# Decode attention beside an MLP on one core: scores by 128-row matmuls, softmax bank by bank, diagonal sums on VectorE

## The chip, the cores and the metric

The kernel runs on 1 core of a Trainium2 chip. Time is the device time of one execution in microseconds (us). Before the change, three runs gave 216.44, 219.92 and 221.33, with a median of 219.92. One execution was recorded by the hardware profiler, and all durations below are from it. Engines are named as in the profile: PE (TensorE), PEld (its weight loads), DVE (VectorE), ACT (ScalarE), POOL (GpSimd), SP (the queue that issues nearly all DMAs).

## The reference

```python
xn = layernorm(x)                                   # x: 4 rows of 576, bf16
# A: decode attention, batch 4, 32 query heads on 16 key heads, window = the last 2048 of 8192 positions
q = (xn @ wq) as 4 x 32 x 128
p = softmax(q @ k^T * 128 ** -0.5) over the window
a = (p @ v) as 4 x 4096 @ wo
# B: MLP; with a sequence of one, the shifted groups g0..g3 are all zero, so x1 = xn
b = xn + gelu(layernorm(xn) @ w3) @ w4              # 576 -> 4608 -> 576
out = x + a + b
```

K and V of the window are 16 heads of 2 MB each. With wq, w3, wo and w4 the kernel reads 87.2 MB and writes 4.5 KB.

## The kernel before

**Layout.** A K or V tile of one head h holds all four batch rows: partition b*32 + p holds 64 consecutive positions (NCH = 64) of batch b, 128 values each. So one load is 128 partitions of 16 KB. K must be turned before it can be contracted over the 128 values: DVE does this with two STREAM_TRANSPOSE per head (line 258), which turn 32x32 blocks of 32-bit words. The result kt has the 128 values of a key spread over four places, the 32 partitions of a group g and the four places y inside, so a score is a sum over four y; the four groups g of 32 partitions hold different keys.

**Scores.** qz holds q for these 32x32 products: per batch b, head h and place y a block of 32 columns that is zero except in the two columns of that head's two query heads. For each head, y and b there are four matmuls (line 267), one for each group g, of 32 rows by 32 columns, each into a bank of its own S[g], rows 32*b and up. So 64 matmuls a head write into the same four PSUM banks for all 16 heads; a row of S[g] is a pair of batch and query head. Nothing of the scores can be read before the last head.

**q.** wq is multiplied by the normalised x in five pieces (line 204) into two PSUM tiles; eight DVE and eight ACT casts (lines 222, 224) put q into q_rows; for each y, eight PE transposes (line 230) go into a PSUM tile tq, and four copies, one for each b, put tq into qz: even b on DVE (line 239), odd b on ACT (line 237). tq has two buffers.

**Softmax.** After the last head of K: a maximum of each bank on DVE (279), Exp of each bank on ACT (283), then four pieces. In each piece E is multiplied by the reciprocal of its row's sum and by a mask of its batch row (300 on ACT, 302 on DVE), turned by PE in two halves (306), and copied from PSUM into PZ, first half on DVE (314), second half on ACT (311).

**V.** For head h, 16 matmuls (line 331) with PZ stationary, 128x32, and V moving, 128x512, fill a bank; four neighbouring key blocks i stand beside each other, so that only the diagonal (i with i) of the four 32x(4*128) row groups counts. ACT copies the bank to osb (line 356). In a later step, `select`, four f32 matmuls against sel pick and add the diagonal (line 362, shown as eight instructions), then DVE casts `on` (366), four small matmuls (369) and two casts `onx` (377) spread the head for wo. After each second head, `project` adds that pair's product with wo to ACC (line 339). `select` and `project` are put into a list `later` and run before the next head's V matmuls.

**MLP.** w3 is multiplied beside the first five heads of K (line 401), gelu follows, and w4's first nine rows of 128 come after K; the remaining 27 come at the end, in loads of 9, 9, 4, 2, 2 and 1 rows (line 419).

**Buffers and order.** SP issues the loads in one queue and waits there for a free buffer. K and V share the pool `kv` with NKV = 6 tiles. The pool `w` has three slots, for pieces of wq, w3, w4 and for E. `kt` has two slots, for kt, q_rows, the softmax pieces and osb. `wo` has three. qz and PZ share one buffer (`pzp`). PSUM has eight banks: ps_tp 1, ps_s 4 (S, before them qp, after them the softmax's transposes), ps_o 2, ps_acc 1. The order of instructions within an engine's queue is set by the framework's planner, from the order in the program, priorities and its own estimate of times; so the order in a trace can differ from the order of the lines. The planner also makes all the waits, and it puts those that touch the same PSUM tile behind one another.

Of the kernel before, what the change touches and what calls it, by code (L numbers as in the profile page):

```python
# [9 lines left out]
ALU = mybir.AluOpType  # L10
# [6 lines left out]
NKV = 6  # L17
# [4 lines left out]
def kernel(  # L22
# [13 lines left out]
):  # L36

# [36 lines left out]
    def ap_of(t, offset_elems, dims):  # L74
        a = t[:]
        return bass.AP(a.tensor, a.offset + offset_elems, [list(a.ap[0])] + [list(d) for d in dims])

    def ap32(t, offset, dims):
        names = " ".join("abcdefg"[:len(t.shape) - 1])
        a = t[:].rearrange(f"p {names} -> p ({names})").bitcast(I32)  # L80
        return bass.AP(a.tensor, a.offset + offset, [list(a.ap[0])] + [list(d) for d in dims])
# [5 lines left out]
    pzp = ctx.enter_context(tc.tile_pool(name="pz", bufs=1))  # L87
# [3 lines left out]
    ps_s = ctx.enter_context(tc.tile_pool(name="ps_s", bufs=4, space=PSUM))  # L91
# [73 lines left out]
    NH = Hkv * rep  # L165
    qz = pzp.tile([P, B, Hkv, NY, NH], BF16, tag="pz", name="qz")

# [7 lines left out]
    nq = B * Hkv * NY * NH // 4  # L175
# [50 lines left out]
    for y in range(NY):  # L226
# [5 lines left out]
        for b in range(B):  # L232
            src = ap_of(tq, b, [[G, 4], [rep * P, 4], [P, rep]])
            step = NY * NH + rep
            dst = ap_of(qz, b * Hkv * NY * NH + y * NH, [[4 * step, 4], [step, 4], [1, rep]])
            if b % 2:
                nc.scalar.copy(out=dst, in_=src)
            else:
                nc.vector.tensor_copy(out=dst, in_=src)
# [10 lines left out]
    S = []  # L250

    def k_scores(h):
# [8 lines left out]
        if h == 0:  # L261
            S.extend(ps_s.tile([P, 512], F32, tag="S", name=f"S{g}") for g in range(NG))
        for y in range(NY):
            e, t = divmod(y, 2)
            for b in range(B):
                for g in range(NG):
                    nc.tensor.matmul(out=S[g][32 * b:32 * b + 32, :].rearrange("p (c k l) -> p c k l", k=GK, l=2),  # L267
                                     lhsT=qz[32 * g:32 * g + 32, b, h, y, :],
                                     rhs=kt[32 * g:32 * g + 32, :, e, b:G:B, :, t],
                                     start=(h == 0 and y == 0), stop=(h == Hkv - 1 and y == NY - 1),  # L270
                                     skip_group_check=True)

    def softmax():
        E = wpl.tile([P, NCH, NG, GK], F32, tag="w", name="E")
        mx = const.tile([P, NG], F32)
        nb = const.tile([P, 1], F32)
        sm = const.tile([P, NG], F32)
        for g in range(NG):
            nc.vector.reduce_max(out=mx[:, g:g + 1], in_=S[g][:], axis=AX.X)  # L279
        nc.vector.reduce_max(out=nb[:], in_=mx[:], axis=AX.X)  # L280
        nc.vector.tensor_scalar_mul(out=nb[:], in0=nb[:], scalar1=-scale)  # L281
        for g in range(NG):
            nc.scalar.activation(out=E[:, :, g, :].rearrange("p (c l) k -> p c k l", l=2),  # L283
                                 in_=S[g][:].rearrange("p (c k l) -> p c k l", k=GK, l=2), func=ACT.Exp, bias=nb[:], scale=scale, accum_out=sm[:, g:g + 1])
        rd = const.tile([P, 1], F32)
        nc.vector.tensor_reduce(out=rd[:], in_=sm[:], op=ALU.add, axis=AX.X)
        nc.vector.reciprocal(out=rd[:], in_=rd[:])
        rdm = const.tile([P, B], F32)
        nc.vector.tensor_scalar_mul(out=rdm[:], in0=mask[:], scalar1=rd[:])  # L289

        PZ = pzp.tile([P, Hkv, NCH, B * rep], BF16, tag="pz", name="PZ")
        HC = CP // 2
        for piece in range(NP):
            c0 = piece * CP
            pr = ktp.tile([P, CP, NG, GK, B], BF16, tag="kt", name=f"pr{piece}")
            for b in range(B):
                src = E[:, c0:c0 + CP, :, :].rearrange("p c g k -> p (c g k)")
                dst = pr[:, :, :, :, b].rearrange("p c g k -> p (c g k)")
                if b == 3 or (b == 1 and piece % 2):
                    nc.scalar.mul(out=dst, in_=src, mul=rdm[:, b:b + 1])  # L300
                else:
                    nc.vector.tensor_scalar_mul(out=dst, in0=src, scalar1=rdm[:, b:b + 1])  # L302
            for half in range(2):
                tp = ps_s.tile([P, HC, P], BF16, tag="S", name=f"pt{piece}{half}")
                for cc in range(HC):
                    nc.tensor.transpose(out=tp[:, cc, :],  # L306
                                        in_=pr[:, half * HC + cc, :, :, :].rearrange("p g k b -> p (g k b)"),
                                        identity=ident[:])
                c1 = c0 + half * HC
                if half:  # L310
                    nc.scalar.copy(out=ap_of(PZ, c1 * B * rep, [[NCH * B * rep, Hkv], [rep, HC * B], [1, rep]]),  # L311
# [119 lines left out]
    for h in range(Hkv):  # L431
# [7 lines left out]
        if h in w3:  # L439
            g_piece(w3.pop(h), h)  # L440
            if h == KJ:
                gelu()
# [63 lines left out]
```

## Time and profile before

| | before |
|---|---|
| median of the three runs, us | 219.92 |
| profiled execution, us | 216.28 |
| its span, us | 214.4 |
| mean granted clock of PE | 0.729 |
| PE busy, us | 129.1 (60%) |
| DVE busy, us | 109.1 (51%) |
| ACT busy, us | 30.3 (14%) |
| moved by DMA | 87.45 MB, 408 GB/s over the span |
| instructions | 4295 |
| K transposes, line 258 | 32 of 2293 ns |
| score matmuls, line 267 | 1024, 36.9 us busy |
| V matmuls, line 331 | 256, 30.1 us busy |
| select matmuls, line 362 | 128, 23.5 us busy |

The span goes from the first to the last instruction of the profiled execution; its time is 1.9 us longer. A line of the table of groups gives the source line, engine, operation, tile written and tiles read, shapes and count, then busy time and the mean of one, then the idle time just before them and what ended it. The slices cut the span into 40 parts of 5.36 us and give busy tenths. The stages by time: q until 33 us, K until 113, softmax until 134.5, V until 205, the rest of w4 until 211.4.

### The profile page before, as it was taken

Reading aid. Unit: us, or ns where it says so; the run is one execution under the profiler, and the core shown is the slowest. Engines: PE = TensorE matmul, PEld = TensorE weight load, DVE = VectorE, ACT = ScalarE, POOL = GpSimd, SP = SyncE. Lnnn points to the kernel's source line nnn. Section 1 sums busy time; section 2 is a strip of 40 time slices with the busy share of each in tenths; the row PEclk is TensorE's granted clock in tenths of the full one; section 3 lists DMA queues with packets and bytes.
Section 4 is the critical chain, followed back from the end, with each engine's and each line's share of the span. In section 5 each row is a group of like instructions: output and inputs, shape, how many; then the busy total and the mean of one; then the engine's idle time right before and its main releaser. Section 6 shows DMA issues by size and latency. Waiting matters only on the chain.

```text
span 214.4 us, 4295 instructions
## 1 busy us (share of the span) xinstructions
PE 129.1 (60%) x1937; PEld 75.8 (35%) x1937; DVE 109.1 (51%) x157; ACT 30.3 (14%) x52; POOL 1.8 (1%) x8
## 2 busy tenths in 40 slices
PE   0343787847644445444534086886777876877694
PEld 0110743526411111111101073555545453545383
DVE  7941968583999999999885493111100000000000
ACT  0201320000000000000002897221111112011200
POOL 1110000000000000000000000000000000000000
PEclk9999999678558587575558569969675558555859
DMA  6999999999999999999999999999999999999980
GB/s 253 433 407 426 426 432 426 415 433 437 411 425 419 437 425 425 419 431 425 413 433 428 428 420 427 424 426 409 432 429 427 419 424 428 431 416 418 422 324 33
DMA packets 8251, 87.45 MB, mean 408 GB/s; under 512 B 924, under 2 KB 1064, under 8 KB 2728
## 3 DMA queue, kind: packets, MB, share of 16 engines
q1 hardware_dynamic: 8216, 87.17, 96.7%
q8 instruction: 15, 0.25, 0.5%
q14 instruction: 4, 0.03, 0.0%
q10 hardware_dynamic: 16, 0.01, 0.0%
HBM read 87.17 MB, written 0.00 MB: 407 GB/s over the span
## 4 chain that ended last, share of the span: by engine, by line
DMA 40%; PE 33%; DVE 15%; ACT 8%; issue 3%; SPq 0%; ACTq 0%; DVEq 0%
DMA t<-in_A_k_cache_dram 36%; PE OT L362 11%; PE O L331 11%; DVE kt L258 6%; PE ACC L339 5%; ACT osb L356 4%; DMA wq<-in_A_wq_dram 3%; PE pt L306 2%; ACT E L283 2%; PE OT L369 2%; DVE qz L177 2%; PE qp L204 1%; ACT PZ L311 1%; ACT pr L300 1%; DVE mx L279 1%
## 5 line engine op out<-in xcount | busy, mean ns | idle before, releaser
L258 DVE STREAM_TRANSPOSE kt<-t 128x2048 int32<-128x2048 int32 x32 | 72.3, 2293 | 12.3 <-DMA t<-in_A_k_cache_dram 12.3
L267 PE MATMUL S<-kt,qz 32*32 32x512 bf16 x1024 | 36.9, 625 | 37.5 <-DVE kt L258 36.1
L366 DVE CAST on<-OT 128x8 bf16<-128x8 f32 x16 | 2.7, 166 | 58.4 <-PE OT L362 58.4
L267 PEld LDWEIGHTS <-qz 32*32 32x32 bf16 x1024 | 10.7, 95 | 60.1 <-issue 56.9
L331 PE MATMUL O<-t,PZ 128*32 128x512 bf16 x256 | 30.1, 506 | 1.1 <-ACT PZ L311 0.6
L362 PE MATMUL OT<-sel,osb 128*128 128x8 f32 x128 | 23.5, 311 | 10.2 <-ACT osb L356 10.1
L362 PEld LDWEIGHTS OT<-sel,osb 128*128 128x128 f32 x128 | 22.1, 260 | 20.5 <-ACT osb L356 20.0
L356 ACT COPY osb<-O 128x512 f32<-128x512 f32 x16 | 9.3, 586 | 59.4 <-PE O L331 59.4
L331 PEld LDWEIGHTS <-PZ 128*32 128x32 bf16 x256 | 10.5, 112 | 8.2 <-issue 3.6
L283 ACT ACTIVATE E<-S,nb 128x512 f32<-128x512 f32 x4 | 4.0, 1115 | 59.4 <-DVE nb L281 59.4
L306 PE MATMUL pt<-ident,pr 128*128 128x128 bf16 x64 | 5.8, 266 | 9.6 <-DVE pr L302 8.6
L401 PEld LDWEIGHTS <-w 128*128 128x128 bf16 x144 | 9.2, 163 | 5.2 <-DMA w<-in_B_w_dram 2.7
L401 PE MATMUL ACC<-ln2T,w 128*128 128x4 bf16 x144 | 9.6, 202 | 1.8 <-DMA w<-in_B_w_dram 1.8
L339 PE MATMUL ACC<-wo,onx 128*4 128x288 bf16 x64 | 8.8, 418 | 2.6 <-DVE onx L377 2.6
L306 PEld LDWEIGHTS <-pr 128*128 128x128 bf16 x64 | 5.0, 122 | 10.9 <-ACT pr L300 10.8
L377 DVE CAST onx<-OT 32x16 bf16<-32x16 f32 x32 | 5.3, 165 | 6.0 <-PE OT L369 5.8
L300 ACT ACTIVATE pr<-E,rdm 128x512 bf16<-128x512 f32 x6 | 8.1, 1434 | 0.7 <-DVE rdm L289 0.7
L204 PE MATMUL qp<-wq,xnT 128*4 128x512 bf16 x32 | 4.0, 620 | 5.1 <-DMA wq<-in_A_wq_dram 5.1
L302 DVE TENSOR_SCALAR pr<-E,rdm 128x512 bf16<-128x512 f32 x10 | 6.5, 797 | 0.3 <-PE pt L306 0.2
L339 PE MATMUL ACC<-w,gT 128*4 128x288 bf16 x72 | 6.6, 341 | 0.0
L224 DVE CAST q_rows<-qp 128x256 bf16<-128x256 f32 x8 | 2.9, 411 | 7.0 <-PE qp L204 7.0
L369 PE MATMUL OT<-on,ident 128*32 128x8 bf16 x64 | 4.2, 172 | 3.6 <-DVE on L366 3.6
(71 smaller groups left out, 64.4 us busy)
## 6 DMA issues: line engine op xcount, KB each, us to landing
t<-in_A_k_cache_dram SPq DMA_DIRECT2D x16, 2048.0 KB, 24.7
t<-in_A_v_cache_dram SPq DMA_DIRECT2D x16, 2048.0 KB, 28.4
w<-in_B_w_dram SPq DMA_DIRECT2D x4, 1152.0 KB, 12.8
wo<-in_A_wo_dram SPq DMA_DIRECT2D x8, 576.0 KB, 18.2
wq<-in_A_wq_dram SPq DMA_DIRECT2D x4, 1024.0 KB, 6.7
w<-in_B_w_dram SPq DMA_DIRECT2D x3, 1296.0 KB, 27.8
w_t<-in_B_w_dram SPq DMA_DIRECT2D x1, 576.0 KB, 14.0
w<-in_B_w_dram SPq DMA_DIRECT2D x1, 576.0 KB, 25.2
```

Of the source, the lines that this page charges most:

```text
L258: nc.vector.transpose(out=ap32(kt, e * G * 2, [[2 * G * 2, NCH // 2], [1, 2], [2, G]]), in_=ap32(kn, e * G, [[2 * 2 * G, NCH // 2], [2 * G ...
L267: nc.tensor.matmul(out=S[g][32 * b:32 * b + 32, :].rearrange("p (c k l) -> p c k l", k=GK, l=2), lhsT=qz[32 * g:32 * g + 32, b, h, y, :], ...
L283: nc.scalar.activation(out=E[:, :, g, :].rearrange("p (c l) k -> p c k l", l=2), in_=S[g][:].rearrange("p (c k l) -> p c k l", k=GK, l=2), ...
L300: nc.scalar.mul(out=dst, in_=src, mul=rdm[:, b:b + 1])
L302: nc.vector.tensor_scalar_mul(out=dst, in0=src, scalar1=rdm[:, b:b + 1])
L306: nc.tensor.transpose(out=tp[:, cc, :], in_=pr[:, half * HC + cc, :, :, :].rearrange("p g k b -> p (g k b)"), identity=ident[:])
L331: nc.tensor.matmul(out=bank[G * j:G * j + G, :], lhsT=PZ[:, h, c0:c0 + NI, :].rearrange("p c m -> p (c m)"), rhs=vn[:, c0:c0 + NI, :].rear ...
L339: nc.tensor.matmul(out=ACC[32 * q:32 * q + B, 0:DH], lhsT=lhsT, rhs=rhs_cols(q * DH, (q + 1) * DH), start=False, stop=False, skip_group_ch ...
L356: nc.scalar.copy(out=osb[:], in_=bank[:])
L362: nc.tensor.matmul(out=OT[:, 0:rep * B], lhsT=osb[:, i * Dh:(i + 1) * Dh], rhs=sel[:, i * rep * B:(i + 1) * rep * B], start=(i == 0), stop ...
L369: nc.tensor.matmul(out=T[0:32, x, :], lhsT=ident[:, x:P:XR], rhs=on[:].rearrange("p r b -> p (r b)"), start=(x == 0), stop=(x == XR - 1), ...
L401: nc.tensor.matmul(out=gp[:, fc, :], lhsT=lhsT, rhs=rhs, start=False, stop=False, skip_group_check=True)
```

## The change

- **Scores.** qz now has, for each b, h and y, a block of 32 columns in which group g's rows are non-zero only in columns 8*g to 8*g+7. One matmul of 128 rows by 32 columns then gives all four groups at once, each in its own eight rows of the output. Eight rows are four heads with two query heads each, so a PSUM bank is one set of four heads (HG = 4) and 512 columns, and 16 matmuls a head take the place of 64. Writing qz takes 16 copies for each y, of 32 partitions each, in the place of four of 128 partitions.
- **Softmax by bank.** A bank of four heads is complete when its last head is scored. Its softmax has three steps: `softmax_exp` (maximum, Exp), `softmax_spread` (reciprocal of the sum, multiply by the masks), `softmax_turn` (16 PE transposes, 16 copies to PZ[bk]). They are called one, two and three heads later in the program; for the last bank they are called before V's heads 0, 1 and 2. A row's keys now stand in four rows (one for each g), so the maximum and the sum go over them by `over_g`: a DVE transpose, a reduce, a broadcast and a transpose back. Multiplies and copies are on ACT for the first three banks and shared with DVE for the last.
- **Diagonal sums.** osb and the four f32 matmuls become four DVE operations from the PSUM bank into osum (128x128), with `diag` as the per-row factor, and one f32 matmul.
- **Memory.** NKV is 5 where it was 6; qz and the PZ[bk] have memory of their own; E and its product share one tile EP in the pool `w`; PSUM has ps_s 2 and a new ps_t with one tile of two banks.

```diff
-NKV = 6
+NKV = 5
...
-    ps_s = ctx.enter_context(tc.tile_pool(name="ps_s", bufs=4, space=PSUM))
+    ps_s = ctx.enter_context(tc.tile_pool(name="ps_s", bufs=2, space=PSUM))
+    ps_t = ctx.enter_context(tc.tile_pool(name="ps_t", bufs=1, space=PSUM))
...
+    HG = 4
+    NB = HG * rep
+    qz = const.tile([P, B, Hkv, NY, G], BF16)
...
-        for b in range(B):
-            src = ap_of(tq, b, [[G, 4], [rep * P, 4], [P, rep]])
-            step = NY * NH + rep
-            dst = ap_of(qz, b * Hkv * NY * NH + y * NH, [[4 * step, 4], [step, 4], [1, rep]])
-            if b % 2:
-                nc.scalar.copy(out=dst, in_=src)
-            else:
-                nc.vector.tensor_copy(out=dst, in_=src)
+        for g in range(NG):
+            p0 = slice(32 * g, 32 * g + 32)
+            for b in range(B):
+                src = ap_of(tq, b, [[G, HG], [rep * P, HG], [P, rep]], p0)
+                dst = ap_of(qz, (b * Hkv * NY + y) * G + NB * g, [[HG * NY * G, HG], [NY * G + rep, HG], [1, rep]], p0)
+                if b % 2:
+                    nc.scalar.copy(out=dst, in_=src)
+                else:
+                    nc.vector.tensor_copy(out=dst, in_=src)
...
+        bk, h4 = divmod(h, HG)
+        if h4 == 0:
+            S[bk] = ps_s.tile([P, 512], F32, tag="S", name=f"S{bk}")
         for y in range(NY):
             e, t = divmod(y, 2)
             for b in range(B):
-                for g in range(NG):
-                    nc.tensor.matmul(out=S[g][32 * b:32 * b + 32, :].rearrange("p (c k l) -> p c k l", k=GK, l=2),
-                                     lhsT=qz[32 * g:32 * g + 32, b, h, y, :],
-                                     rhs=kt[32 * g:32 * g + 32, :, e, b:G:B, :, t],
...
+                nc.tensor.matmul(out=S[bk][32 * b:32 * b + 32, :].rearrange("p (c k l) -> p c k l", k=GK, l=2),
+                                 lhsT=qz[:, b, h, y, :], rhs=kt[:, :, e, b:G:B, :, t],
+                                 start=(h4 == 0 and y == 0), stop=(h4 == HG - 1 and y == NY - 1),
+                                 skip_group_check=True)
+
+    def over_g(col, op, last):
+        t1 = small.tile([P, G], F32, tag="og1")
+        nc.vector.transpose(out=t1[:].bitcast(I32), in_=col[:].bitcast(I32))
+        r = small.tile([P, NB], F32, tag="og2")
+        nc.vector.tensor_reduce(out=r[:], in_=t1[:].rearrange("p (g m) -> p m g", m=NB), op=op, axis=AX.X)
+        t2 = small.tile([P, NG, NB], F32, tag="og3")
+        last(t2, r[:].unsqueeze(1).to_broadcast([P, NG, NB]))
+        t3 = small.tile([P, G], F32, tag="og4")
+        nc.vector.transpose(out=t3[:].bitcast(I32), in_=t2[:].rearrange("p g m -> p (g m)").bitcast(I32))
+        return t3[:, 0:1]
...
+    def softmax_exp(bk):
+        nc.vector.reduce_max(out=cols[0][:, 0:1], in_=S[bk][:], axis=AX.X)
+        nb = over_g(cols[0], ALU.max, lambda t, r: nc.vector.tensor_scalar_mul(out=t[:], in0=r, scalar1=-scale))
+        EP = wpl.tile([P, 512 + NCH * GK * B // 2], F32, tag="w", name=f"EP{bk}")
...
+        nc.scalar.activation(out=SM[bk][0].rearrange("p (c l k) -> p c k l", l=2, k=GK),
+                             in_=S.pop(bk)[:].rearrange("p (c k l) -> p c k l", k=GK, l=2),
+                             func=ACT.Exp, bias=nb, scale=scale, accum_out=cols[1][:, 0:1])
+
+    def softmax_spread(bk):
+        E, pr = SM[bk]
+        rd = over_g(cols[1], ALU.add, lambda t, r: nc.vector.tensor_copy(out=t[:], in_=r))
...
+        for b in range(B):
+            if bk < Hkv // HG - 1 or b == 3:
+                nc.scalar.mul(out=pr[:, :, b], in_=E, mul=rdm[:, b:b + 1])
+            else:
+                nc.vector.tensor_scalar_mul(out=pr[:, :, b], in0=E, scalar1=rdm[:, b:b + 1])
+
+    def softmax_turn(bk):
...
+        tp = ps_t.tile([P, NCP, P], BF16, tag="T", name=f"pt{bk}")
+        for c in range(NCP):
+            nc.tensor.transpose(out=tp[:, c, :], in_=prc[:, c * P:(c + 1) * P], identity=ident[:])
+        PZ[bk] = const.tile([P, HG, NG, NCP, NB], BF16, name=f"PZ{bk}")
+        n = 0
+        for i in range(NG):
+            for g in range(NG):
+                pi, po = slice(32 * i, 32 * i + 32), slice(32 * g, 32 * g + 32)
+                if bk == Hkv // HG - 1 and n % 3 < 2:
+                    nc.vector.tensor_copy(
...
                 else:
+                    nc.scalar.copy(
...
-        osb = ktp.tile([P, NI * Dh], F32, tag="kt", name=f"osb{h}")
-        nc.scalar.copy(out=osb[:], in_=bank[:])
+        osum = ktp.tile([P, Dh], F32, tag="kt", name=f"osum{h}")
+        nc.vector.tensor_scalar_mul(out=osum[:], in0=bank[:, 0:Dh], scalar1=diag[:, 0:1])
+        for i in range(1, NI):
+            nc.vector.scalar_tensor_tensor(out=osum[:], in0=bank[:, i * Dh:(i + 1) * Dh], scalar=diag[:, i:i + 1],
+                                           in1=osum[:], op0=ALU.mult, op1=ALU.add)
...
-            for i in range(NI):
-                nc.tensor.matmul(out=OT[:, 0:rep * B], lhsT=osb[:, i * Dh:(i + 1) * Dh],
-                                 rhs=sel[:, i * rep * B:(i + 1) * rep * B],
...
+            nc.tensor.matmul(out=OT[:, 0:NB], lhsT=osum[:], rhs=sel[:], start=True, stop=True, skip_group_check=True)
...
+        for d, step in enumerate((softmax_exp, softmax_spread, softmax_turn), 1):
+            if h >= d + HG - 1 and (h - d) % HG == HG - 1:
+                step(h // HG - 1)
...
-    PZ = softmax()
+    steps = [softmax_exp, softmax_spread, softmax_turn]
     for v in range(Hkv):
...
+        if steps:
+            steps.pop(0)(Hkv // HG - 1)
         v_compute(v)
```

## The prediction

> **What bounds the kernel now.** I read the page's slices first. They show which resource is full from end to end.
>
> ```profile
> DVE  7941968583999999999885493111100000000000
> ACT  0201320000000000000002897221111112011200
> PEclk9999999678558587575558569969675558555859
> DMA  6999999999999999999999999999999999999980
> GB/s 253 433 407 426 426 432 426 415 433 437 411 425 419 437 425 425 419 431 425 413 433 428 428 420 427 424 426 409 432 429 427 419 424 428 431 416 418 422 324 33
> ```
>
> The 16 DMA engines are full from the second slice to the last but one, at some 425 GB/s. The 20 us from 114 to 134 in which DVE and ACT make the softmax and PE does little are no dip in that row: V is loading then. 87.45 MB at 425 GB/s are 205.8 us of a span of 214.4. What is left is 2 us before the first packets, an uneven last 4 us, and 3 us from the last packet to the end. A faster engine therefore earns nothing in the middle; what counts is whether a wait ever lets the DMA queue run empty, and what follows the last byte.
>
> Next the chain of waits in order of time, for the second half.
>
> ```profile
> 134.55 0.41 PE O L331 x2
> ...
> 192.97 0.59 ACT osb L356
> 193.56 0.04 issue
> 193.61 1.89 PE OT L362 x8
> ...
> 205.64 5.74 PE ACC L339 x60
> 211.40 0.45 DVE fin L473
> ```
>
> From 134.5 to 211.4 PE and its hand-overs to ACT and DVE run without one wait for a transfer. So there are two bounds at par: the stream, and a PE chain that starts 20 us late. The windows by 1 us show how near they are:
>
> ```profile
> 209.00:210.00 1.00, 1.00 (x17) 0.96 (x14) 0.00 (x0) 0.00 (x0) 0.00 (x0) 0.79 0.38 144
> 210.00:211.00 1.00, 1.00 (x21) 0.99 (x18) 0.00 (x0) 0.00 (x0) 0.00 (x0) 1.00 0.09 31
> 211.00:212.00 1.00, 0.35 (x6) 0.03 (x1) 0.45 (x1) 0.00 (x0) 0.00 (x0) 1.00 0.00 0
> ```
>
> The last columns are granted clock, DMA share and GB/s: bytes move until 210 to 211 (the last w4 load, issued at 195.05, lands 15.8 us later, at 210.9), and the last matmul that needs them starts at 211.1. PE is at most 0.5 us behind.
>
> **The V stage on PE.** The timeline has an osb copy at 178.46 and one at 188.09, two heads apart: 9.63 us per pair. The stream needs 2 x 2048 + 576 KB = 4.78 MB per pair, 11.2 us at 427 GB/s. The edit: osb (0.59) becomes four DVE operations on 128x128 (nearest rows: 128x144 copy from PSUM 0.27, two-input 128x144 0.31), 1.1 to 1.25 per head, +1.3 per pair at the upper end; the 8 f32 L362 instructions, 1.06 in one head of a pair and 1.88 in the other by the granted clock, become 2, 0.27 and 0.47: -2.2. New pair: 8.7 us, under 11.2. V also starts some 18 us earlier, so PE is going to wait for V, with the stream the only bound.
>
> The granted clock in this stage is 0.54 to 0.66 by 10 us windows with PE 75% busy, and 0.50 in the slow stretches. If all of it ran like the slow heads, before's pair would grow by 0.82 (L362) and 1.1 (the 16 L331, 0.92 against 1.76 for twelve) to 11.6: over the stream. Its PE has no spare time at the end, so that comes through whole: an execution that got a colder clock would be up to 8 x 1.9 = 15 us longer. The medians fit this: 219.92 and 221.33 stand 3.6 and 5.0 over the profiled 216.28. The new pair in such a run is 8.7 + 0.2 + 1.1 = 10.0, still hidden.
> The Trainium skill (TensorE: Matmul & The Clock Gate, Part 1) says that an array left idle for a window of about 3.4 us falls back to half clock. That speaks against a change that lets PE wait for V; by it every new pair is the 10.0 one, by the trace's mixture 8.7.
>
> **The K stage.** Scores: 64 matmuls a head on 32x32 become 16 on 128x32 like L331 (16 take 1.2 to 2.3 us), before 2 x 1.13; PE waits 36 us for DVE there, so nothing comes of it. DVE is what is near its limit: 4.51 us of transposes per head against 4.9 between K tiles. The rows:
>
> ```profile
> L258 DVE STREAM_TRANSPOSE kt<-t 128x2048 int32<-128x2048 int32 x32 | 72.3, 2293 | 12.3 <-DMA t<-in_A_k_cache_dram 12.3
> L356 ACT COPY osb<-O 128x512 f32<-128x512 f32 x16 | 9.3, 586 | 59.4 <-PE O L331 59.4
> L300 ACT ACTIVATE pr<-E,rdm 128x512 bf16<-128x512 f32 x6 | 8.1, 1434 | 0.7 <-DVE rdm L289 0.7
> ```
>
> Each of three banks adds to DVE a maximum (L279, 0.68) and ten small operations; 0.16 to 0.23 each by L280 to L289 (small 32-column transposes have no row: between the slope of L258, 1.1 ns per column, 0.04, and a 128x128 reduce, 0.30; I take 0.16). About 2.5 us a bank, 2 to 4. Idle time from 58 us on is 5.1 us for two of them: DVE ends K at most 1 to 3 us later (112.6 before), and this is bought back many times by the softmax that leaves. ACT gets, per bank, Exp 1.3, four L300 = 5.7 and 16 copies of 32x512 (L356, and half of L311's 1.07: 0.53 to 0.59) = 9: 16 us in the 19.6 of four heads. It was idle. If ACT were late, PE would wait for its transposes and K tiles pile up; three queued tiles (15 us) cover that.
>
> **Buffers.** NKV 6 to 5: load n waits for tile n-5. When that tile is transposed, or used by V, three later ones are still queued, 15 us of stream against 1.3 us from an issue to the first bytes (the first load is issued at 0.73; the window from 1 to 2 us moves 50 GB/s, the next 315). I cost it at nothing (0 to 1 us). Before, after V5 was issued at 116.1 the next V load waited for V0's use until 135; now V0 is used some 4 us after it lands at about 113. EP takes w slots; the slots w4 needs were used by banks that are long done. The last bank's 16 copies alternate engines on one tile: 11 x 0.4 + 5 x 0.56 = 7 us and hand-overs, 8.5 at most; only head 12 needs them, 60 us later, and the heads held up meanwhile have 15 us of V in the queue.
>
> **The start.** q's copies are the one place where the new work can starve the stream.
>
> ```profile
> 29.69 0.19 DVE L239 COPY qz<-tq 128x32 bf16<-128x32 bf16 x1 [1.22 <-PE tq L230]
> 29.91 0.19 ACT L237 COPY qz<-tq 128x32 bf16<-128x32 bf16 x1 [1.23 <-DVE qz L239]
> 30.13 0.19 DVE L239 COPY qz<-tq 128x32 bf16<-128x32 bf16 x1 [0.25 <-ACT qz L237]
> 30.36 0.19 ACT L237 COPY qz<-tq 128x32 bf16<-128x32 bf16 x1 [0.26 <-DVE qz L239]
> ```
>
> Copies from one tq tile wait for each other in turn, 0.215 apart; two tq tiles side by side at 27.77 gave 0.115. 16 copies become 64, so 48 more: 5.6 to 10.3 us. K0's scores then end at 40 to 45 and not at 34.8, and with them g_piece(1) and the load of w3_t and K5 behind it on SP's queue, issued at 38.78. By then SP has issued 19.92 MB; the first seven slices moved 15.02 MB by 37.5, so the rest lasts 11.5 us, to 49.0. Spare: 10.2, less 1.3 to the first bytes. At 5.6 nothing is lost; at 10.3, 1.4 us. I take 0, keeping 1.4 as an end.
> The Trainium skill (PSUM — Partial Sum Buffer, Terms) says that different 32-partition quadrants of one bank may be accessed at the same time. The new copies go by quadrants, so by it they need not alternate and, as an estimate, 24 of 0.18 us on each of two engines add 4.3 us; the trace shows only whole-height copies, and those take turns.
>
> **The sum.** Instruction loads (queue 8) take 0.5% of 16 engines' span, 1.07 us for 4295 instructions. 768 matmuls and 768 weight loads of the scores and 192 of L362 go, some 150 small ones come: 37% fewer, -0.4. PE's lag behind the last load: -0.2 (0 to -0.5). Span 214.4 - 0.6 = 213.8; with the 1.9 that the profiled time has over its span, **215.7**. This stands 0.3% under the profiled 216.28 and 1.9% under the median of 219.92, for if the stream alone sets the time, runs should come together there. A difference of about 2% is what a measurement of this kernel can tell from none; this forecast lies on that edge.
>
> **Rivals.**
> - The spread is the stream's (a GB/s that varies between executions) and not the clock's. Then PE's spare time buys nothing and the median stays: 219.92 - 0.6 = 219.3. For it: single slices differ by 7%. Against it: over 10 us windows of the V stage the rate is within 417 to 427.
> - Slower: the planner sets K transposes of 2.3 us between the alternating q copies, as it did at 30.65 and 32.95. Each holds up DVE's half of the chain. The chain is 10.3 us longer with none; the stream loses from 8.9 us on, 1 us for each us, so +2% (224.3, 8.6 over the forecast) needs 17.5 us: three to four more transposes inside the chain. With those, 224 to 228. Against it: g_piece(1) waits for neither q nor K and may be placed ahead, and then w3_t's load isn't late at all.
> - It doesn't do what it says: a bank's transposes on PE stand ahead of the next scores and wait for ACT, DVE waits for kt buffers, and the stream starves in K. A stall must outlast 15 us; ACT's whole work for a bank is 16. 217 to 223.
>
> **How the numbers follow.** Floor: 0.70, 213.2 to 217.5; I give 0.41 of it under 215.5 and 0.29 above, as a colder clock no longer counts. Stream spread: 0.10, within 2%. Starved in K: 0.06, nearly all within 2%. Start starved: 0.14, slower by over 2%. So faster 0.42, same 0.43, slower 0.15; the cut runs through the likeliest case. Its own range is 213.2 to 217.5. To leave out no more than 2 in 10 the range goes down to 213 and up to 222.5, which takes in 219.3, the 1.4 of the start and most of the starved K.
>
> **What would show it.** Right: DMA slices full to the end as before; in the V stage O matmuls of L331's successor waiting for V loads; DVE in K without idle time for DMA in the last heads; osum about 1.2 us a head; a last matmul within 0.3 us of the last load. Wrong: a DMA slice under 380 GB/s near 45 to 55 us (the start), near 70 to 110 (K), or after 115 (buffers); V matmuls still without waits for transfers; runs spread as widely as before.

## The result, and the profile after

| | before | after |
|---|---|---|
| median, us | 219.01 (216.44 to 221.33, 6 runs) | 228.06 (226.44 to 229.09, 6 runs) |
| ratio after to before | | 1.0455, 95% interval 1.0377 to 1.0532 |
| profiled execution / span, us | 216.28 / 214.4 | 226.44 / 224.7 |
| instructions | 4295 | 2738 |
| last K transpose ends, us | 112.64 | 123.45 |
| V head 0 is in PSUM, us | 134.97 | 137.84 |
| the fourth wo load, wo(3), is issued, us | 144.29 | 154.92 |

The kernel became slower by 4.6%; forecast were 215.7 us and 213.0 to 222.5. Ratios, here and below, leave out executions that are over 1.5% above the fastest of the same kernel, so they can differ a little from the ratio of the medians.

V0 to V15 are the V tiles of the 16 heads, wo(0) to wo(7) the pieces of wo for a pair of heads each, K2 the third K tile. The page's slices of the changed kernel (one slice is 5.62 us; the rows are those shown of before):

```profile
DVE  7933959793999797978799245754425252333420
ACT  0202241102749302769356970310000000000000
PEclk9999999967557855557555875556955575555758
DMA  6999999999999999999999996962999999999970
GB/s 250 448 407 442 406 434 424 433 422 429 424 420 426 438 432 423 423 423 425 430 435 429 404 426 228 381 283 57 431 398 439 415 444 410 442 411 435 415 302 6
```

Everywhere else the stream is as full as before; slices 25 to 28, from 135 to 157 us, have 228, 381, 283 and 57 GB/s. The windows by 10 us give the size of the hole (columns: length; busy time and instructions of PE, PEld, DVE, ACT, POOL; granted clock; DMA share; GB/s):

```profile
130.00:140.00 10.00, 4.26 (x34) 2.60 (x35) 4.94 (x14) 3.61 (x5) 0.00 (x0) 0.58 0.78 317
140.00:150.00 10.00, 4.59 (x43) 2.01 (x42) 7.12 (x22) 2.88 (x5) 0.00 (x0) 0.50 0.92 366
150.00:160.00 10.00, 5.66 (x60) 3.42 (x60) 4.64 (x17) 0.00 (x0) 0.00 (x0) 0.73 0.44 164
```

Against 425 GB/s these three lack 2.5, 1.4 and 6.1 us of streaming, 10.1 together. The span is 10.3 longer: by its size the hole accounts for the whole loss.

Why was nothing loaded? The timeline of SP's queue in after, behind V4 (123.48) and wo(2) (124.08):

```profile
137.88 5.00 SPq L101 DMA_DIRECT2D t<-in_A_v_cache_dram  x2
154.92 0.33 SPq L375 DMA_DIRECT2D wo<-in_A_wo_dram  x1
155.31 1.19 SPq L101 DMA_DIRECT2D t<-in_A_v_cache_dram  x2
```

V5 has to wait for the buffer of V0, until 137.88. The first `x2` line is V5 and V6. Then comes wo(3), which takes the buffer of the first wo tile and so waits for `project` of heads 0 and 1; in this trace PE does that behind V head 3 (first line below). V7 stands behind wo(3) in the queue and had to wait with it. In the trace of before the same wo(3) (second line) was issued 10.6 us earlier, the loss once more.

```profile
153.65 1.24 PE L367 MATMUL ACC<-wo,onx 128*4 128x288 bf16 x8
...
144.29 0.33 SPq L347 DMA_DIRECT2D wo<-in_A_wo_dram  x1
```

Of these 10.6 us, 2.9 are V0's own delay (137.84 against 134.97). The rest arose between V0's first sum or copy and wo(3): 17.0 us in after (137.89 to 154.92), 9.3 in before (135.03 to 144.29).

What made V's first heads late is in the chain of waits, here from 130 to 138 us (start, length, what):

```profile
130.45 0.58 ACT PZ L338
131.05 1.18 ACT EP L302 x2
...
133.67 1.94 DVE EP L318 x3
135.74 0.27 PE pt L327
136.01 1.83 PE O L359 x16
```

V0 needs only bank 0, which was ready 60 us before. But the Exp of the **last** bank stands behind the 16 copies of bank 2 in ACT's queue, as its timeline shows:

```profile
121.62 9.41 ACT L338 COPY PZ<-pt 32x512 bf16<-32x512 bf16 x16 [1.98 <-PE pt L327]
```

The multiplies of the last bank wait for it, its first transpose (135.74) waits for them, and V0's 16 matmuls stand behind that transpose in PE's queue. After V0 the last bank's copies take DVE in turns with V's diagonal sums, as the timeline of DVE shows:

```profile
144.15 0.35 DVE L386 SCALAR_TENSOR_TENSOR osum<-O,diag,osum 128x128 f32<-128x128 f32 x1
144.53 0.42 DVE L334 COPY PZ<-pt 32x256 int32<-32x256 int32 x1
144.99 0.35 DVE L386 SCALAR_TENSOR_TENSOR osum<-O,diag,osum 128x128 f32<-128x128 f32 x1
```

So heads 0 to 3 end at 137.8, 142.3, 149.1 and 153.9.

The table of groups has, for the three rows that the prediction showed of the K stage, these in after:

```profile
L266 DVE STREAM_TRANSPOSE kt<-t 128x2048 int32<-128x2048 int32 x32 | 71.6, 2283 | 0.9 <-PE S L275 0.9
L338 ACT COPY PZ<-pt 32x512 bf16<-32x512 bf16 x53 | 30.6, 577 | 17.6 <-DVE PZ L334 10.9
L316 ACT ACTIVATE EP<-EP,rdm 128x512 bf16<-128x512 f32 x13 | 16.2, 1423 | 14.5 <-DVE rdm L313 14.5
```

The transposes are as many and as long as before, but the 12.3 us in which they waited for K's bytes are gone: DVE, not the stream, sets the pace of K. ACT is busy for 46.8 us in these two groups and stands 14.5 us waiting for DVE's small operations ahead of the second.

### The profile page after: what moved, and what is told of

It is laid out like the page before. It is cut to its first block, busy times and chain, and to the rows that moved or that the text cites. A ratio compares the mean times of both kernels' runs of the same rounds, so it can differ in the third digit from the quotient of the medians.

```text
span 224.7 us, 2738 instructions
## 1 busy us (share of the span) xinstructions
PE 116.3 (52%) x1073; PEld 61.4 (27%) x1073; DVE 139.4 (62%) x283; ACT 60.8 (27%) x116; POOL 1.8 (1%) x8
## 4 chain that ended last, share of the span: by engine, by line
DVE 40%; PE 24%; DMA 15%; ACT 13%; issue 7%; SPq 0%; ACTq 0%; DVEq 0%
DVE kt L266 20%; DMA w<-in_B_w_dram 11%; PE O L359 7%; ACT PZ L338 5%; PE S L275 4%; ACT EP L316 4%; DVE osum L386 4%; PE ACC L367 4%; DMA wq<-in_A_wq_dram 3%; PE pt L327 3%; PE OT L392 3%; ACT EP L302 2%; DVE PZ L334 2%; DVE qz L180 2%; DVE osum L384 1%
## 5 line engine op out<-in xcount | busy, mean ns | idle before, releaser
L275 PE MATMUL S<-kt,qz 128*32 128x512 bf16 x256 | 35.7, 632 | 35.8 <-DVE kt L266 29.3
L338 ACT COPY PZ<-pt 32x512 bf16<-32x512 bf16 x53 | 30.6, 577 | 17.6 <-DVE PZ L334 10.9
L275 PEld LDWEIGHTS <-qz 128*32 128x32 bf16 x256 | 8.5, 110 | 54.7 <-issue 38.1
L384 DVE TENSOR_SCALAR osum<-O,diag 128x128 f32<-128x128 f32 x16 | 5.6, 351 | 26.1 <-PE O L359 26.0
L392 PE MATMUL OT<-sel,osum 128*128 128x8 f32 x32 | 8.3, 333 | 25.7 <-DVE osum L386 25.7
L316 ACT ACTIVATE EP<-EP,rdm 128x512 bf16<-128x512 f32 x13 | 16.2, 1423 | 14.5 <-DVE rdm L313 14.5
L327 PE MATMUL pt<-ident,EP 128*128 128x128 bf16 x64 | 7.9, 310 | 19.7 <-ACT EP L316 10.7
L386 DVE SCALAR_TENSOR_TENSOR osum<-O,diag,osum 128x128 f32<-128x128 f32 x48 | 16.8, 351 | 1.7
L392 PEld LDWEIGHTS OT<-sel,osum 128*128 128x128 f32 x32 | 7.2, 280 | 36.8 <-issue 35.3
L327 PEld LDWEIGHTS <-EP 128*128 128x128 bf16 x64 | 6.4, 143 | 24.6 <-ACT EP L316 22.9
L359 PEld LDWEIGHTS <-PZ 128*32 128x32 bf16 x256 | 11.2, 120 | 6.7 <-issue 5.2
L394 DVE CAST on<-OT 128x8 bf16<-128x8 f32 x16 | 2.7, 167 | 10.6 <-PE OT L392 10.5
L241 ACT COPY qz<-tq 32x32 bf16<-32x32 bf16 x32 | 5.1, 179 | 10.6 <-DVE qz L243 9.8
```

What stands on the lines that cost most here:

```text
L275: nc.tensor.matmul(out=S[bk][32 * b:32 * b + 32, :].rearrange("p (c k l) -> p c k l", k=GK, l=2), lhsT=qz[:, b, h, y, :], rhs=kt[:, :, e, ...
L316: nc.scalar.mul(out=pr[:, :, b], in_=E, mul=rdm[:, b:b + 1])
L327: nc.tensor.transpose(out=tp[:, c, :], in_=prc[:, c * P:(c + 1) * P], identity=ident[:])
L338: nc.scalar.copy(out=ap_of(PZ[bk], i * NCP * NB, [[NG * NCP * NB, HG], [rep, NCP * B], [1, rep]], po), in_=ap_of(tp, g * NB, [[rep, HG], [ ...
L359: nc.tensor.matmul(out=bank[G * j:G * j + G, :], lhsT=PZ[bk][:, h4, j, s * NI:(s + 1) * NI, :].rearrange("p c m -> p (c m)"), rhs=vc[:, j, ...
L384: nc.vector.tensor_scalar_mul(out=osum[:], in0=bank[:, 0:Dh], scalar1=diag[:, 0:1])
```

## The experiments

Each kernel is compared with executions of the kernel before on the same chip. The chips differ between groups of experiments, so two changed kernels are best compared by their ratios. The table gives the instants that the reading above makes decisive, from each profile; the texts refer to it.

| | ratio (95%) | last K transpose | first sum or osb copy of V0 | wo(3) issued | GB/s 130-140, 140-150, 150-160 |
|---|---|---|---|---|---|
| before | 1 | 112.64 | 135.03 | 144.29 | 426, 419, 427 |
| after | 1.0455 | 123.45 | 137.89 | 154.92 | 317, 366, 164 |
| a1 | 1.0500 (1.0430-1.0571) | 123.56 | 137.99 | 154.93 | 431, 273, 129 |
| a2 | 1.0553 (1.0476-1.0631) | 123.99 | 135.93 | 151.40 | 427, 275, 308 |
| a3 | 1.0252 (1.0175-1.0330) | 123.59 | 127.75 | 141.16 | 427, 424, 422 |
| a5 | 1.0226 (1.0163-1.0290) | 123.64 | 138.11 | 152.65 | 310, 394, 251 |
| a6 | 1.0113 (1.0073-1.0153) | 115.27 | 130.86 | 147.88 | 429, 302, 435 |
| c1 | 0.9940 (0.9901-0.9980) | 115.47 | 119.62 | 132.84 | 430, 426, 421 |
| c2 | 0.9843 (0.9790-0.9895) | 115.74 | 119.89 | 132.81 | 429, 426, 423 |
| b4 | 0.9866 (0.9814-0.9917) | 111.54 | 133.95 | 142.16 | 438, 428, 422 |

### Buffers: five tiles instead of six (b1, a1)

b1 is the kernel before with `NKV = 5`. a1 is the changed kernel with six tiles; the room comes from letting each PZ lie in the part of qz that its bank no longer needs:

```diff
-NKV = 5
+NKV = 6
-    qz = const.tile([P, B, Hkv, NY, G], BF16)
+    qz = const.tile([P, Hkv // HG, B, HG, NY, G], BF16)
...
-        PZ[bk] = const.tile([P, HG, NG, NCP, NB], BF16, name=f"PZ{bk}")
+        PZ[bk] = qz[:, bk].rearrange("p b h y n -> p (b h y n)").rearrange("p (h g c m) -> p h g c m", h=HG, g=NG, c=NCP)
```

> The kernel before with NKV = 5 and nothing else. Buffer theory (the sixth tile is what the changed kernel lacks at the switch from K to V): the stream loses one tile, 4.9 us or more, so 1.02 to 1.05 of before. Hold-up theory (what is lost hangs on when V's first heads are used): by 134 us before's stream had 3.1 MB or 7.3 us still queued; one tile less leaves 2.4 us, so it runs dry for 0 to 1 us: 1.00 to 1.005.

> The changed kernel with six K and V tiles (PZ[bk] is put where qz's block of that bank was, which frees the room). Buffer theory: the sixth tile gives 4.9 us or more back, 216 to 222. Hold-up theory: V5 goes out 14 us earlier, but V7 stands on SP behind wo3, which waits for project of heads 0 and 1 at 154.9; the same bytes are issued before 154.9, so the dry time only moves together: within 1 us of the changed kernel, ratio 1.04 to 1.05. K-late theory (DVE ends K 11 us later, and that is the loss): no change either.

b1 measured 218.13 against 217.88, 1.0005 (0.9958 to 1.0052). a1 measured 227.95. With a tile more, the bytes move into the hole's first third (431 GB/s instead of 317), and the rest of the hole grows by as much, for wo(3) is issued at 154.93 as in after. The missing sixth tile is no cause; wo(3) is the gate.

### The last bank out of V's way (a2, a3)

a2 moves only the last bank's transposes on PE (and its copies) behind V head 3; a3 moves all three steps of the last bank, behind V heads 2, 4 and 6:

```diff
-    steps = [softmax_exp, softmax_spread, softmax_turn]
+    steps = {2: softmax_exp, 4: softmax_spread, 6: softmax_turn}
...
-        if steps:
-            steps.pop(0)(Hkv // HG - 1)
         v_compute(v)
         head_out(v)
+        if v in steps:
+            with tc.issue_after(v_last[v].ins), tc.issue_after(o_last[v].ins):
+                steps[v](Hkv // HG - 1)
```

> The changed kernel, with the PE transposes of the last bank put behind V head 3 in PE's order; maximum, Exp and spreading of that bank stay where they are on DVE and ACT. Hold-up theory: V0 is used at 127 to 129 instead of 136 to 138, V5 goes out at 129; but osum of head 0 still stands on DVE behind bank 3's Exp, until 135.6, so project of heads 0 and 1 and wo3 come at about 148, and the stream is dry for some 5 us instead of 10: 221 to 224, ratio 1.015 to 1.03. K-late theory: DVE's end of K is the same, so no change, 1.04 to 1.05.

> The changed kernel with all three steps of the last bank's softmax put behind V's heads 2, 4 and 6 on DVE and PE. Hold-up theory: V0 used at 129, its osum at 131, project of heads 0 and 1 and wo3 at about 139, before the stream is dry at 145: the whole 10 us come back, 215.5 to 219, ratio 0.985 to 1.00. K-late theory: K still ends at 123.5 on DVE, so the time stays at 1.04 to 1.05. Buffer theory: still five tiles, so no more than half comes back.

a2 missed: 228.97. V0's matmuls were done at 127.9, 10 us earlier, and V5 was issued at 127.93, but V0's sum waited on DVE for the last bank, whose small transposes wait for the Exp on ACT:

```profile
132.80 0.21 DVE L283 STREAM_TRANSPOSE t<-cols 128x32 int32<-128x32 int32 x1 [4.94 <-ACT EP L302]
...
135.93 0.33 DVE L386 TENSOR_SCALAR osum<-O,diag 128x128 f32<-128x128 f32 x1
```

So taking one engine out of the knot leaves the next: the wait moved from PE's queue to DVE's, and the copies then came between heads 4 and 5.

a3 measured 222.83. The stream has no hole any more, as expected, and yet less than half of the expected gain came (0.985 to 1.00 was expected): V0's sum begins 8 us later than in c1 below (127.75 against 119.62), since K ends at 123.6; the last bank's copies hold DVE from 159.5 to 167.7; and the loop, at 10.60 us for two heads (osum at 184.40 and 195.00), ends with head 15's matmuls at 210.1, when the bytes have all landed. PE's w4 rows then take until 218.7; the end was PE's, not the stream's.

### Is it the V loop? (a4, b2, a5)

a4 gives the changed kernel its osb copy and four f32 matmuls back; b2 gives the kernel before the diagonal sums alone:

```diff
-        osum = ktp.tile([P, Dh], F32, tag="kt", name=f"osum{h}")
-        nc.vector.tensor_scalar_mul(out=osum[:], in0=bank[:, 0:Dh], scalar1=diag[:, 0:1])
...
+        osb = ktp.tile([P, NI * Dh], F32, tag="kt", name=f"osb{h}")
+        nc.scalar.copy(out=osb[:], in_=bank[:])
```

a5 keeps the changed kernel's work and puts `select` and `project` of a head behind the V matmuls of the next one in PE's queue:

```diff
-        run_later()
         v_compute(v)
+        with tc.issue_after(v_last[v].ins):
+            run_later()
         head_out(v)
```

> The changed kernel with osb on ACT and the four f32 matmuls back. V-loop theory: pairs at 9.6 to 11, and DVE has only the last bank's copies in the first heads: 3 to 7 us back, ratio 1.01 to 1.035. Rival (switch alone): V0 is used at 136 all the same, ratio 1.04 to 1.05.

> The kernel before with only the diagonal sums moved: four DVE operations and one f32 matmul for osb and four f32 matmuls. V-loop theory (the loop PE O, DVE osum, PE OT, DVE on, PE runs at 10.6 us a pair with PE at half clock, as the changed kernel's trace has it, against 9.63 before): V0 is done at 135 as before, 15 heads at 5.3 end at 214.5 and not at 202.6, so 1.035 to 1.055. Rival (V's loop is hidden behind the stream, the loss comes from the switch from K to V alone): 1.00.

> The changed kernel with select and project of head v put on PE behind the V matmuls of head v+1, so that osum runs beside them. V-loop theory: a head costs PE some 3.7 us and DVE 2.1, under the stream's 5.6; the hole in the stream at 135 to 156 stays for the most part (V0 still waits for bank 3's first transpose until 136), but no chain outlasts the stream: 1.015 to 1.035. Rival: 1.04 to 1.05.

a4: 1.0534 (1.0444 to 1.0623), from executions of 228.75 and 230.42; b2: 218.13 against 217.36, 0.9977 (0.9922 to 1.0031). Both expectations of a guilty V loop missed: with the sums undone the loss stays, and with the sums alone there is none. a5: 222.43, 1.0226 where after has 1.0455, so some 5 us less, with three quarters of the hole left (310, 394 and 251 GB/s lack 7.5 us). The rest of its gain is behind the hole: PE no longer waits there for each head's sums on DVE, and after 156 us its chain of waits goes from transfer to transfer. So the sums don't make the loss, but the loop in the order as written can't win anything back either.

### Why is K late? (a6)

In after the planner puts a bank's maximum on DVE ahead of K transposes that could run while the scores for it are still being made; the small operations that wait for Exp stand ahead of transposes likewise. a6 sets each step behind the calling head's K transposes:

```diff
-                step(h // HG - 1)
+                with tc.issue_after(k_last[h].ins):
+                    step(h // HG - 1)
```

> The changed kernel with each bank's maximum and sum put on DVE behind the K transposes of the head in whose place the program calls them, so that DVE doesn't stand waiting for PE's scores and ACT's Exp. DVE's time per bank falls from 23.5 to about 20.6, so K ends at 114 to 117 instead of 123.5. ACT's own round of a bank (Exp 1.4, spread 4.9, copies 9.4, and the waits between them) stays at 20 to 23 us, so the last bank's Exp comes at 126 to 131 and V0, behind its first transpose on PE, at 131 to 136. Hold-up theory: 0 to 4 us back, 1.025 to 1.045. K-late theory: 6 to 9 us back, 1.005 to 1.02.

Measured 220.30, 1.0113: by the ratios some 7.5 us under after, the largest recovery by one edit, and in the range given for a late K. The timeline of DVE for one bank of after has two stalls inside the K stage (in brackets the idle time and what ended it):

```profile
85.42 0.21 DVE L283 STREAM_TRANSPOSE t<-cols 128x32 int32<-128x32 int32 x1 [1.29 <-ACT EP L302]
...
101.84 0.69 DVE L298 TENSOR_REDUCE cols<-S 128x1 f32<-128x512 f32 x1 [1.99 <-PE S L275]
```

and of a6, in the same place, none:

```profile
85.83 13.48 DVE L268 STREAM_TRANSPOSE kt<-t 128x2048 int32<-128x2048 int32 x6
99.23 0.65 DVE L300 TENSOR_REDUCE cols<-S 128x1 f32<-128x512 f32 x1
```

From 42 to 123 us DVE of after waits 9.4 us for scores and Exp, that of a6 0.2. The Exps of banks 1 and 2 begin 23.6 us apart in after (84.22, 107.82) and 20.6 in a6 (82.66, 103.22). K ends at 115.27, 2.6 us behind before; V0 is done 7.0 earlier than in after, and the whole rest shifts with it (wo(3) -7.0, span -7.4). A hole remains in one window (302 GB/s), since the last bank's Exp still stands behind bank 2's copies on ACT, at 124.02.

### All of it together (c1, c2, c3)

c1 is a6 and a3 together, c2 is c1 with a5's order, c3 is c2 with each turned q tile copied by one engine (`y % 2` where it was `b % 2`).

> The two recoveries together: the three steps of the bank's softmax put behind the calling head's K transposes on DVE, and the last bank's three steps behind V heads 2, 4 and 6. Theory (the time is lost because V's first head comes late and the stream's V and wo loads hang on it; the loop behind it is too slow to win it back): K's transposes end at about 115 as in a6_k_order, V0's matmuls at about 119.5 (a3_bank3_after_v had 127.7 with K ending at 123.5), the last head's 82.4 later as in a3_bank3_after_v, at about 202, under the stream's end. No slice of the stream under 390 GB/s before the last two; 214.5 to 218, ratio 0.98 to 0.998. Rival (the V loop with diagonal sums on DVE is over the stream by itself, wherever it starts): last head's matmuls at 207 to 210, 219 to 222, ratio 1.005 to 1.02. Second rival (the two recoveries are the same microseconds): 220 to 221, as a6_k_order alone.

> c1 with select and project of a head put behind the V matmuls of the next one, so that PE doesn't wait for DVE's sums. Theory: the V loop then waits for the stream alone and the floor that the prediction named is reached: 213.5 to 216, ratio 0.97 to 0.99; if c1 is at the stream already, the two are within 1 us. Rival (V loop over the stream by itself): 2 to 5 us under c1, as a5_select_late was under after by 5.

> c2 with all the copies of one turned q tile on one engine (y even ACT, y odd DVE), instead of alternating within the tile. If the taking of turns delays K's beginning (K2's transposes 5.8 us later in after than before) and that delay comes through, it is 1 to 4 us under c2; if three tiles queued ahead cover it or the V stage is at the stream, within 1 us of c2.

c1: 216.53 (214.99 to 217.66). V0 at 119.6 and the end of head 15's matmuls at 203.7, near what the theory had (119.5 and 202); PE's remaining rows end at 212.0, 3 us behind the last bytes. c2: 215.29 (215.02 to 215.46): 1.6% under the kernel before, a small gain, but the interval leaves 1 out; the instructions are those of the slow version. The rate in its slices has no hole left:

```profile
GB/s 240 442 399 438 413 433 429 420 436 414 430 433 428 417 433 433 420 430 430 412 435 433 430 405 434 427 430 413 430 420 433 418 427 419 431 423 432 414 357 16
```

and its chain of waits in the V stage reads:

```profile
155.19 1.90 PE O L364 x16
...
158.46 19.11 DMA t<-in_A_v_cache_dram
177.61 1.90 PE O L364 x16
```

The V stage now goes from transfer to transfer; four heads take 22.42 us (155.19 to 177.61, and 22.43 to the next at 200.04), 11.2 for two. c3: 215.28, 0.9841 (0.9785 to 0.9898), the same as c2: who copies q is worth nothing.

### Which part earns it? (b3, b4, c2 again)

b3 gives the kernel before a5's order alone; b4 gives it a5's order and the diagonal sums, with the softmax still after K. c2 ran again beside b4.

> The kernel before with select and project put behind the V matmuls of the next head, nothing else. If before's median stands over its best execution because the PE chain of the V stage is at par with the stream and an execution with a colder clock is over it (the prediction's reading), the chain's share goes: 215 to 217.5, ratio 0.98 to 0.995. If the spread is the stream's (the prediction's first rival), nothing is gained: 0.997 to 1.003.

> The kernel before, softmax still after K, with the two edits of the V stage alone: diagonal sums on DVE, select and project behind the next head's V matmuls. Theory (what the best order of the changed kernel gains is the V stage's and the tail's, and the earlier start of V is worth nothing by itself, since the stream was never short of room): V still begins at about 131 to 135, the loop waits for the stream, the last V head lands at about 201 as in b3_before_select_late, and the tail behind it is 10.5 us as in c2_and_select_late instead of 13.9: span 214.7, 216 to 217, ratio 0.985 to 0.993. Rival (the softmax beside K is what pays, through V's start): as before or b3_before_select_late, ratio 0.997 to 1.006.

> The best order of the changed kernel once more, beside the one above, for a narrower interval: 215 to 215.6, ratio 0.98 to 0.99. If the earlier start of V is worth nothing by itself, the two are within 1.5 us; if it is what pays, they are 2.5 us or more apart.

b3: 219.50 against 218.48, 1.0053 (1.0005 to 1.0100): no gain, against the first expectation; the interval touches the second (0.997 to 1.003). V's last tile lands at 201.03 and V waits for transfers, but what is left for PE behind it takes until 214.90. From the timeline of PE in b3:

```profile
203.81 1.88 PE L364 MATMUL OT<-sel,osb 128*128 128x8 f32 x8
...
206.87 1.88 PE L364 MATMUL OT<-sel,osb 128*128 128x8 f32 x8
```

Two heads' f32 selects at half clock (1.88 each; the one f32 matmul behind the sums takes 0.60 in c2's tail) and w4's rows come behind the last tile, and the clock stays at 0.50 until after 212.

b4: 214.28 (213.69 to 215.22) against 217.22, 0.9866 (0.9814 to 0.9917). c2 again: 215.03 (214.72 to 215.20), 0.9897 (0.9844 to 0.9950). The end of b4's chain:

```profile
187.94 20.26 DMA w<-in_B_w_dram
208.24 0.65 PE ACC L346 x6
208.91 0.45 DVE fin L481
```

DVE's last operation ends 1.2 us behind the last transfer. (The ratio is the one expected; the time is under the 216 to 217 given: the last head's matmuls began at 199.07 and not at about 201, and from there to DVE's last operation it took 9.8 us and not 10.5, with PE's clock at 1.00 from 203 on.) V0 is at 133.95 there, 14 us later than in c2, and the time is no longer: 214.28 beside 215.03. So the softmax beside K, with the scores that allow it, is worth nothing in time here; the gain is the V stage's, and there neither edit alone shows one (b2 0.9977, b3 1.0053), but the two together do. The margin is narrow: b2's interval begins at 0.9922, b4's ends at 0.9917, and they ran on different chips.

## Why the prediction was wrong, step by step

- **The bound.** Right, and it explains both the loss and what the reordered kernels reach: the stream at 425 GB/s with nothing to spare. c2 and b4 reach 215.3 and 214.3, where 215.7 was forecast for a kernel that the stream alone sets. What the prediction did with it was too short: it looked for a dry queue at the start, in K and at the buffers, and not at the switch from K to V.
- **"V also starts some 18 us earlier ... now V0 is used some 4 us after it lands at about 113": the step that failed.** V0's matmuls were done at 137.84, 2.9 later than before. The data allow an early V0 (c1 to c3 have it done at 119 to 120); the queues as written don't. The prediction costed which bank a head needs, and not what stands ahead of it on ACT, DVE and PE. It had seen the wait itself: its part on buffers says that before's next V load waits for V0's use until 135, and takes this as gone.
- **The last bank's copies, "only head 12 needs them".** The same mistake: true of the data, but they lie in DVE's queue between the sums of heads 0 to 2, 139.58 to 149.4, and delay `project` and wo(3). The stated cover, "15 us of V in the queue", wasn't there, as SP waited for exactly those heads. Of the 17.0 us from V0's first sum to wo(3) the copies are some 4: a3 and c1, which have them later, take 13.4 and 13.2. What makes up the rest over the 9.3 of before isn't separated by a run; the sums alone bring b2 to 10.9 (134.39 to 145.27), and PE's granted clock from 130 to 150 was 1.00 and 0.83 in before, 0.58 and 0.50 in after.
- **"DVE ends K at most 1 to 3 us later".** Right for the operations: 2.6 us with the order of a6. But 10.8 as written; the 8.2 between the two fit the 9.4 us that DVE waits for scores and Exp, which the sum didn't have. ACT's work for a bank was near the 16 us given (1.17 + 0.21, 4.9, 9.4 by the rows of after, 15.7), but its round was 23.6 and not 19.6, with waits of 5.76 for DVE and 1.98 for PE between its parts. That "three queued tiles (15 us) cover that" held for the stream inside K, and not for V0, at the end of the line.
- **The V pair.** 8.7 us was said for the clock of before and 10.0 at half clock; measured 10.61 at half clock (osum at 168.08 and 178.69) and 9.55 in the next pair. The base was a favourable one: osb copies of before, two heads apart from 157.63 to 199.39, give pairs of 9.53, 11.30, 9.63 and 11.30, and the prediction took the 9.63; the mean of the four is 10.4. Of the excess over 10.0 the sums are most: they take 1.51 a head from first to last, four of 0.35 with gaps, where 1.1 to 1.25 was said. The new pairs stay under 11.2, as was said, but only 0.6 to 1.7 a pair is left to recover a late start.
- **"The Trainium skill (TensorE: Matmul & The Clock Gate, Part 1)"** spoke against letting PE wait. By 10 us windows the clock hardly differs: 0.54 to 0.66 in before from 160 to 210, 0.50 to 0.67 in after from 160 to 220, and 0.50 to 0.70 in c2 from 140 to 210, where PE waits for V's transfers and loses nothing by it. The tail behind the last V tile is another matter: from the last head's first matmul to the last DVE operation c2 takes 10.5 us, with the clock at 0.50 until 208, and b4 9.8, with 1.00 from 203 on.
- **The spread between executions**, read as the PE chain's and not the stream's: borne out. Where the stream sets the time, ten executions of c2 lie between 214.72 and 215.46 and six of b4 between 213.69 and 215.22, while before ranged from 215.78 to 221.33 over all its executions. That the clock is what varies the PE chain is not shown: of the executions of before beside the experiments, the 36 with a mean granted clock of 0.72 or more have a median of 217.1 us and reach 220.1, the 16 under 0.70 have 217.6 and reach 221.3. What was wrong was to think that any relief of PE brings the spread down: b2 and b3 each relieve it and gain nothing.
- **Buffers** "at nothing": right (b1, a1). **The start** "at 0": right; w3_t was issued at 36.27, earlier than before, K2's transposes began at 41.76 instead of 35.95, no slice fell, and c3 shows no cost. The new q copies still took turns (ACT waited 9.8 us for DVE's), so what the Trainium skill (PSUM — Partial Sum Buffer, Terms) says of quadrants had no play in this program. **The instructions** fell by 36%, where 37% was said.
- **The rivals.** "It doesn't do what it says" had the right parts (transposes ahead on PE, ACT's 16 us) but put the hunger into the K stage and bounded it by 223. No rival has SP's loads hang on V's first heads. The list of signs did name a slice under 380 after 115 us, for buffers; the sign came, for another reason.

Not shown: why the planner orders a bank's steps as it does, and how much of a6's recovery is the stalls on DVE and how much the Exp and transposes that they hold up on ACT and PE in turn.

## What to carry to other kernels

When a load queue is full with nothing to spare, ask of each load what must be done before it may be issued, and follow that through every engine's queue: an operation whose result nobody needs for a long time still stops what stands behind it. Here work moved beside a full stream gained nothing by starting earlier, and its order decided whether it cost 4.6% or nothing; the same instructions gave 228 and 215 us. Where a PE chain is at par with the stream, try taking it off the wait path and shortening what it leaves for the end together, for here either alone gave nothing.

## What the runs showed of the hardware that was not expected

- PE stayed at half clock (a granted clock of 0.50) for long while busy. In b3, windows of 3 us from 203 to 212 have PE busy for 2.74, 3.00 and 3.00 us at a granted clock of 0.50, and 0.71 in the next; in c2 the clock is 0.50 from 200 to 208, with PE busy for 7.70 of these 8 us. In b4 it rose some 3 us after the last V tile's matmuls began (0.50 in 199 to 201, 0.76, then 1.00). The Trainium skill (TensorE: Matmul & The Clock Gate, Part 1) puts the rise after some 3.4 us of sustained work; b4 fits that and b3 and c2 don't. Busy time counts matmuls that are small or wait on their weights, so how much the array itself worked isn't seen.
- The sum's DVE operations, 128x128 f32 with the bank in PSUM, take 351 ns each (L384 and L386 of after), where the prediction went by 270 to 310 from copies and two-input operations of 128x144.
